# First k as plain f32, ReLU in DRAM token order, whole-tile stores: a Nystrom attention and squared-ReLU MLP kernel

## The chip, the cores and the metric

The kernel runs on one core of a Trainium2 chip. Its engines each run their own queue of instructions in order and wait for each other through semaphores: TensorE (PE, matmuls and their weight loads), VectorE (DVE), ScalarE (ACT), GpSimd (POOL) and SyncE (SP, which only issues transfers). PE writes into PSUM (8 banks of 2 KB for each of 128 partitions); DVE and ACT carry results from PSUM to the on-chip memory SBUF; DMA engines move data between DRAM and SBUF. Transfers can be issued from the queues of POOL, SP and ACT; only those from POOL's queue change the type on the way (f32 in DRAM to bf16 in SBUF) in this kernel.

The metric is the time of one execution in microseconds (us) on the device. Before the change it is 260.24 us, the median of three runs.

## The reference

Eight batches of eight heads, 576 tokens, head width 64. Nystrom attention with 32 landmarks, then an MLP with a squared ReLU:

```python
q_lm = q.reshape(B, H, m, S // m, D).mean(axis=3)
k_lm = k.reshape(B, H, m, S // m, D).mean(axis=3)
A  = sm(q, k_lm)        # sm: softmax of scale * a @ b^T
Bm = sm(q_lm, k_lm)
C  = sm(q_lm, k)
Z  = Bm.transpose(0, 1, 3, 2) / (norm1(Bm) * norminf(Bm) + 1e-06)
for _ in range(6):
    Z = 2 * Z - Z @ Bm @ Z
x = (A @ Z @ C @ v)     # heads side by side: (4608, 512)
h = x @ w_in            # (512, 2048)
r = np.maximum(h, 0.0)
out = (r * r) @ w_out   # (2048, 512)
```

All inputs and the output are f32; the kernel computes in bf16 with f32 sums.

## The kernel before

Everything is unrolled. The code adds each operation to a plan with its engine choices, and a table of numbers, `ORDER`, then emits the operations: each positive number names one operation, its engine and its PSUM bank; each negative one a run of matmuls of zeros (`fill`, L395), which compute nothing and keep TensorE running while it would wait. So the order of the instructions on every engine, and the choice between DVE and ACT, stand in that table alone; no cost is looked at when the kernel is built.

For each batch `attention(b)` and then `mlp_in(b)` and `mlp_out(b)` are planned, and the table interleaves the attention of the next batch with the MLP of this one. The parts and their lines:

- Loads. `load` (L333) brings q, k or v of a batch as bf16 through POOL's queue, with 96 partitions: partition p holds tokens 6p to 6p+5. `load_w_in` (L341) and `load_w_out` (L349) bring four pieces each of the weights on the same queue. k and q of batch 0 are its first two entries.
- Batch 0 and 1: k and q are transposed on TensorE (L521, evicted as `kqT`), later ones by a DMA transpose on SP's queue (L422).
- Landmarks: batch 0 by 24 matmuls with `seg` for each of k and q (L438), evicted as `kpart` and `qpart` (L273/L275) and folded (L451); later ones by L475.
- Bm and its softmax (L543 or L546, L559, L563, L567, L569), its transpose (L571) and scale (L586 to L592), the start `st` (L611, L613), six steps of a product on TensorE (L634 for batch 0, L639 later) and an update on DVE (L650), the last one into `zt` or `Zd` (L665, L658).
- C: products L679, row maximum L685, exponential L690 into `EC`, transposed (L702 for batch 0 and 1) into `ECT`; C times v (L730); with Z it gives `WT`.
- A: products L781, maximum and difference (`mxA` L790, `SA` L793), exponential L799 into `EA`, sums L805, scaling L816, transposed into `AT`.
- G = `WT` with w_in (L852), copied to SBUF; then the MLP: h from `AT` and G (L872, 4 matmuls of 288 columns for each of 16 blocks f), ReLU from PSUM into `r` (ACT L888 or DVE L890), its square into `gs` (ACT L897 or DVE L899), the output product (L936, 16 matmuls of 512 columns for each tile of 128 tokens), a copy to one of five buffers `o`, and the store to DRAM.

The columns of AT, `r` and `gs` stand in the order (c, p): column 96c + p is token 6p + c. A tile of 128 columns is therefore 128 tokens of which neighbours lie six rows apart in `out`, and it crosses from one c to the next: `store` (L911) issues two transfers for each tile (32 and 96 rows, or 64 and 64), all on SP's queue. The last tile is made in two halves of 256 columns.

```python
def relu(e, hk=hk, r=r):
    rj = r.rearrange("p (j t) -> p j t", j=2)
    src = two(hk)[:, :, 0:HALF]
```

Of the kernel before, what the change touches and what calls it, by code (L numbers as in the profile page):

```python
# [8 lines left out]
P = 128  # L9
# [5 lines left out]
F32 = mybir.dt.float32  # L15

B = 8
H = 8
# [216 lines left out]
def kernel(  # L235
# [111 lines left out]
    def load_w_out(j, gate=()):  # L347
# [8 lines left out]
        act_func_set_id=LN_EXP_SET, name=nc.get_next_instruction_name(),  # L356
        engine=mybir.EngineType.Activation, ins=[], outs=[]))

    load("k", 0)
    load("q", 0)  # L360

    seg = sb.tile([TP, M], BF16, name="seg")
# [553 lines left out]
    def mlp_out(b):  # L916
# [6 lines left out]
        for t, (sk, x0, pieces) in enumerate(tiles):  # L923
# [6 lines left out]
            for hp in range(parts2):  # L930
                for lo, hi in cuts:
# [19 lines left out]
                    if last:  # L951
                        store(osb, ("ob", on, lo), pieces, lo, hi)
# [52 lines left out]
```

## Time and profile before

| | us |
|---|---|
| median of 3 runs (260.06 to 263.48) | 260.24 |
| the profiled execution, whole | 258.97 |
| its span, first to last instruction | 257.3 |
| from the span's start to the first matmul that is not of zeros | 7.6 |
| from there to the first product of the MLP (L872) | 22.7 |
| from there to the last matmul | 222.2 |
| from there to the end of the span | 4.8 |

The granted clock of TensorE is 1.0 throughout. The profile is of one execution; the times of the table after the second row are cut out of its span. A busy share is an average over stages with different limits, so the stages are looked at one by one: ahead of the MLP the chain of batch 0 runs from engine to engine, in the long stage TensorE is busy nearly all the time, and at the end only stores are left. The DMA share of a stretch can be above 1, since reads and writes of the same engine overlap.

### The profile page before, as it was taken

How to read it: one execution, taken by the hardware profiler on the slowest of the kernel's cores; microseconds unless marked ns; L12 is line 12 of the kernel's file. 1: busy time of each engine (PE TensorE's matmuls, PEld its weight loads, DVE VectorE, ACT ScalarE, POOL GpSimd, SP SyncE). 2: the span in 40 equal slices, each digit the busy share in tenths (PEclk: the TensorE clock that was granted, in tenths of full speed). 3: DMA queues.
4: the chain of work that ended last, by engine and by line, in shares of the span. 5: the costliest groups of instructions: out<-in, count | busy, mean ns of one | idle time of the engine just before them, and what ended most of it. 6: DMA issues, size and time to landing. Idle time of an engine off the chain costs nothing.

```text
span 257.3 us, 7197 instructions
## 1 busy us (share of the span) xinstructions
PE 248.2 (96%) x2914; PEld 143.9 (56%) x2914; DVE 183.7 (71%) x423; ACT 179.1 (70%) x357; POOL 83.3 (32%) x127
## 2 busy tenths in 40 slices
PE   8988999999999999999999999999999999999992
PEld 3755645664655466546655665466645555555551
DVE  2396886779779988797578987766987676664400
ACT  1378999789954899786965895789697576454221
POOL 6253915415156224413351347225513220000000
PEclk9999999999999999999999999999999999999999
DMA  6999999799999999999979999999885108000425
GB/s 82 203 204 207 206 208 203 119 166 158 207 184 182 198 215 163 186 211 178 189 152 195 200 189 175 199 143 200 157 119 121 35 16 195 1 23 1 143 63 143
DMA packets 73345, 39.46 MB, mean 153 GB/s; under 512 B 46048, under 2 KB 68832, under 8 KB 73312
## 3 DMA queue, kind: packets, MB, share of 16 engines
q0 software_dynamic: 23040, 18.35, 47.7%
q1 hardware_dynamic: 50272, 20.65, 41.2%
q8 instruction: 23, 0.38, 0.5%
q14 instruction: 10, 0.08, 0.1%
HBM read 36.70 MB, written 9.44 MB: 179 GB/s over the span
## 4 chain that ended last, share of the span: by engine, by line
PE 77%; DMA 10%; DVE 4%; issue 3%; POOL 2%; ACT 2%; POOLq 0%; DVEq 0%; ACTq 0%
PE ps L936 43%; PE ps L872 21%; DMA kqraw<-in_k_dram 5%; DMA kqraw<-in_q_dram 5%; PE ps L852 3%; PE ps L475 2%; PE ps L781 2%; PE ps L730 1%; PE ps L639 1%; PE ps L521 1%; PE ps L395 1%; POOL EA L816 1%; ACT EC L690 1%; POOL Pd L578 1%; PE ps L492 1%
## 5 line engine op out<-in xcount | busy, mean ns | idle before, releaser
L936 PE MATMUL ps<-w_out_bf,gs 128*128 128x512 bf16 (+1 forms) x592 | 148.8, 374 | 0.0
L872 PE MATMUL ps<-AT,G 128*128 128x288 bf16 x512 | 79.1, 286 | 0.1
L936 PEld LDWEIGHTS <-gs 128*128 128x128 bf16 x592 | 53.9, 98 | 44.1 <-issue 5.2
L888 ACT ACTIVATE r<-ps 128x576 bf16<-128x576 f32 x84 | 53.5, 654 | 20.0 <-PE ps L872 13.1
L872 PEld LDWEIGHTS <-G 128*128 128x128 bf16 x512 | 49.0, 98 | 25.2 <-issue 0.7
L578 POOL TENSOR_TENSOR Pd<-st,ones_d 128x256 bf16<-128x256 bf16 x42 | 28.6, 682 | 79.6 <-DVE st L650 59.7
L897 ACT ACTIVATE gs<-r 128x576 bf16<-128x576 bf16 x70 | 45.5, 681 | 6.9 <-DVE r L890 6.5
L890 DVE TENSOR_SCALAR r<-ps 128x576 bf16<-128x576 f32 x44 | 32.7, 749 | 14.2 <-PE ps L872 10.4
L899 DVE TENSOR_TENSOR gs<-r 128x576 bf16<-128x576 bf16 x58 | 28.0, 498 | 3.6 <-ACT r L888 3.2
L267 ACT CAST G<-ps 128x512 bf16<-128x512 f32 x47 | 25.7, 590 | 6.5 <-PE ps L852 6.0
L267 ACT COPY o<-ps 128x512 f32<-128x512 f32 (+1 forms) x19 | 10.8, 576 | 15.6 <-PE ps L936 15.5
L650 DVE SCALAR_TENSOR_TENSOR st<-st,ps 128x128 bf16<-128x128 bf16 x40 | 11.3, 282 | 13.0 <-PE ps L639 8.0
L816 POOL TENSOR_TENSOR EA<-EA,rA 96x384 bf16<-96x384 bf16 x20 | 17.6, 890 | 8.8 <-DVE st L650 6.4
L269 DVE COPY o<-ps 128x512 f32<-128x512 f32 (+1 forms) x18 | 12.1, 669 | 10.3 <-PE ps L936 10.3
L790 DVE TENSOR_REDUCE mxA<-ps 96x16 f32<-96x512 f32 x24 | 16.1, 678 | 3.5 <-ACT gs L897 1.7
L793 DVE TENSOR_TENSOR SA<-ps,mxA 96x512 f32<-96x512 f32 x24 | 16.2, 680 | 0.3
L395 PE MATMUL ps<-zero 128*128 128x512 bf16 (+5 forms) x52 | 14.3, 400 | 1.3 <-DVE zero L401 1.3
L805 DVE TENSOR_REDUCE sA<-EA 96x24 f32<-96x768 bf16 x16 | 15.0, 940 | 0.4 <-ACT EA L799 0.3
L799 ACT ACTIVATE EA<-SA 96x512 bf16<-96x512 f32 x24 | 14.5, 626 | 0.7 <-DVE SA L793 0.7
L269 DVE CAST G<-ps 128x512 bf16<-128x512 f32 x17 | 11.4, 684 | 2.9 <-PE ps L852 2.5
L690 ACT ACTIVATE EC<-ps,nmc 128x576 bf16<-128x576 f32 x16 | 11.9, 744 | 2.1 <-DVE nmc L685 2.0
L685 DVE TENSOR_REDUCE nmc<-ps 128x1 f32<-128x576 f32 x16 | 11.8, 749 | 1.0 <-PE ps L679 1.0
(109 smaller groups left out, 237.4 us busy)
## 6 DMA issues: line engine op xcount, KB each, us to landing
kqraw<-in_k_dram POOLq DMA_DIRECT2D x8, 576.0 KB, 7.2
kqraw<-in_q_dram POOLq DMA_DIRECT2D x8, 576.0 KB, 11.5
vraw<-in_v_dram POOLq DMA_DIRECT2D x8, 576.0 KB, 9.0
out_dram<-o SPq DMA_DIRECT2D x23, 192.0 KB, 2.6
out_dram<-o SPq DMA_DIRECT2D x24, 128.0 KB, 2.5
w_in_bf<-in_moe_w_in_dram POOLq DMA_DIRECT2D x4, 512.0 KB, 9.8
w_out_bf<-in_moe_w_out_dram POOLq DMA_DIRECT2D x4, 512.0 KB, 10.6
out_dram<-o SPq DMA_DIRECT2D x23, 64.0 KB, 2.1
```

What stands on the lines that cost most here:

```text
L267: nc.scalar.copy(dst, src)
L269: ENG[e].tensor_copy(dst, src)
L395: mm(ps[:, bank, 0:64 * w], lhsT=zero[:, 0:P], rhs=zero[:, 0:64 * w], start=True, stop=True)
L578: ENG[e].tensor_tensor(dst[:], src.unsqueeze(2).to_broadcast([P, 2, NG, M]), ones_d[:].unsqueeze(1).to_broadcast([P, 2, NG, M]), ALU.mult)
L793: add({"DVE": dve(512)}, lambda e, sa=sa, j=j: nc.vector.tensor_tensor(grouped(SA[:, j, :]), grouped(one(sa)[0:TP, :]), mxA[:, j, :].unsqu ...
L816: ENG[e].tensor_tensor(w, w, rA[:, i, cs, :].rearrange("p c g -> p (c g)").unsqueeze(2) .to_broadcast([TP, NJ * NG, M]), ALU.mult)
L872: mm(t[:, j, 0:HALF], lhsT=G[:, i, f * P:(f + 1) * P], rhs=AT[:, i, j * HALF:(j + 1) * HALF], start=(i == 0), stop=(i == 1))
L888: nc.scalar.activation(rj, src, AF.Relu)
L890: nc.vector.tensor_scalar(out=rj, in0=src, scalar1=0.0, scalar2=None, op0=ALU.max)
L897: nc.scalar.activation(dst, r[:], AF.Square)
L899: nc.vector.tensor_tensor(dst, r[:], r[:], ALU.mult)
L936: mm(one(ok)[:, 0:hi - lo], lhsT=gs[:, f, x0:x0 + P], rhs=w_out_bf[:, f, lo:hi], start=(f == f0), stop=(f == f1 - 1))
```

## The change

It has four parts and a new table.

1. k of batch 0 is no longer POOL's first load. SP issues it as plain f32 in two halves of four heads each, into memory that `gs` uses later (`kf`); four casts of 96x768 make the bf16 `kqraw` of it, two on DVE and two on ACT. The landmark means of batch 0 (`means`) are split into halves of four heads, and the means and transposes of k wait only for their half. q of batch 0 becomes POOL's first load.
2. ReLU writes `r` with a stride: column 6t + 3j + c instead of (j, c, t), which is the order of tokens in DRAM. The square, `gs` and the output product then run over that order unchanged. The elements that one instruction writes one after another now stand 12 bytes apart.
3. A tile of 128 tokens is 128 neighbouring rows of `out`, and `store` issues one transfer for it.
4. For the last two tiles the table may also choose ACT's queue for a store; it does so once.

```diff
-    load("k", 0)
+    kf = gs.rearrange("p f s -> p (f s)")[0:TP, 0:2 * H * NC6 * D].bitcast(F32).rearrange(
+        "p (h c d) -> p h c d", h=H, c=NC6)
+
+    for y in range(2):
+        def load_kf(e, y=y):
+            nc.sync.dma_start(kf[:, 4 * y:4 * y + 4], k[0, 4 * y:4 * y + 4].rearrange("h (p c) d -> p h c d", c=NC6))
+
+        add({"SP": (450.0,)}, load_kf, writes=[("kf", y)], dma=(2.0 * H * S * D, 460.0, 700.0))
     load("q", 0)
+    for y in range(4):
+        def k_cast(e, y=y):
+            copy(e, kqraw[:, 0, 2 * y:2 * y + 2, :, :], kf[:, 2 * y:2 * y + 2])
+
+        add({"DVE": dve(768), "ACT": act(768, True)}, k_cast, reads=[("kf", y // 2), ("k", 0)], writes=[("kc", y)])
+    FIRST = {"k": [[("k", 0), ("kc", 2 * y), ("kc", 2 * y + 1)] for y in range(2)], "q": [[("q", 0)]] * 2}
...
-                add({"PE": pe(32, 24)}, means, reads=[(nm, 0), "seg"], writes=[mp], acq=("n", mp))
...
+                    add({"PE": pe(32, 12)}, means, reads=FIRST[nm][y] + ["seg"], writes=[mp],
+                        acq=None if y else ("n", mp))
...
-                    add({"PE": pe(TP, 12)}, tr, reads=[(nm, 0), "ident"], writes=[tp], acq=("h", tp))
+                    add({"PE": pe(TP, 12)}, tr, reads=(FIRST[nm][hf] if b == 0 else [(nm, 0)]) + ["ident"],
+                        writes=[tp], acq=("h", tp))
...
             def relu(e, hk=hk, r=r):
-                rj = r.rearrange("p (j t) -> p j t", j=2)
-                src = two(hk)[:, :, 0:HALF]
+                rj = r.rearrange("p (t j c) -> p j c t", j=2, c=NJ)
+                src = two(hk)[:, :, 0:HALF].rearrange("p j (c t) -> p j c t", c=NJ)
...
-    def store(osb, key, pieces, lo=0, hi=DM):
...
-                    nc.sync.dma_start(rows[a:a + m, tok, lo:hi], osb[p0:p0 + m, lo:hi])
...
+    def store(osb, key, row, lo=0, hi=DM, ends=False):
+        def go(e):
+            ENG[e].dma_start(out[row:row + P, lo:hi], osb[:, lo:hi])
...
-                store(osb, ("ob", on, 0), pieces)
+                store(osb, ("ob", on, 0), row, ends=b == B - 1 and t > 2)
```

The table is new from its first number to its last:

```diff
-    136, 24, 64, 104, 176, -1280, 880, 802, 928, 404, 448, 856, -197, 480, 528, -117, 962, 1040, 1016, 224, 608, 4344,
...
+    32, 336, 128, 72, 176, 104, 208, 256, 304, -640, 1080, 1128, 424, 602, -171, 640, 688, 1164, 1208, 376, -99, 722,
...
```

Three places of the order follow. The first is the start of ACT's queue before (`kqT_69` and `kqT_70` are the transposed k and q of batch 0 and of batch 1, `EC_99` and `EA_108` those of batch 0):

```order
L355 ACT_TABLE_LOAD
L267 COPY kqT_69<-ps 128x1152
L273 ACTIVATE kpart<-ps 128x256
L267 COPY kdup<-ps 128x256
L267 COPY kbd<-kdup 64x8x32
L267 COPY qdup<-ps 128x256
L563 ACTIVATE Eb,rs<-ps,nmb 128x32 x2
L799 ACTIVATE EA_108<-SA 96x2x2x128
L690 ACTIVATE EC_99,rsc<-ps,nmc 128x6x96 x2
```

And ACT's queue with the change, in the same place:

```order
L353 ACT_TABLE_LOAD
L265 COPY kqraw<-gs 96x768 x2
L265 COPY kqT_69<-ps 128x1152
L271 ACTIVATE kpart<-ps 128x256
L265 COPY kqT_69<-ps 128x1152
L271 ACTIVATE qpart<-ps 128x256
L265 COPY qdup<-ps 128x256
L265 COPY kqT_69<-ps 128x1152
L577 ACTIVATE Eb,rs<-ps,nmb 128x32 x2
L704 ACTIVATE EC_99,rsc<-ps,nmc 128x6x96 x2
```

The two casts of k (`kqraw<-gs`) came in ahead of everything; ACT now evicts three of batch 0's four transposes instead of one and `qpart` instead of `kdup`, and two of these evictions stand between `kpart` and `Eb`.

The second place is DVE's queue between the softmax of Bm of batch 0 and its first update (`st_93<-st_92`), before:

```order
L685 TENSOR_REDUCE nmc<-ps 128x1 x2
L567 RECIPROCAL rr<-rs 128x2
L790 TENSOR_REDUCE mxA<-ps 96x16
L569 TENSOR_TENSOR BB<-Eb,rr 128x64
L790 TENSOR_REDUCE mxA<-ps 96x16
L793 TENSOR_TENSOR SA<-ps,mxA 96x512
L571 STREAM_TRANSPOSE BTf<-BB 128x64
L793 TENSOR_TENSOR SA<-ps,mxA 96x512
L584 TENSOR_REDUCE cs<-BTf 128x2
L586 TENSOR_REDUCE mx<-cs 128x2
L589 TENSOR_SCALAR cc<-mx 128x2
L592 RECIPROCAL rc<-cc 128x2
```

And with the change:

```order
L699 TENSOR_REDUCE nmc<-ps 128x1 x2
L581 RECIPROCAL rr<-rs 128x2
L583 TENSOR_TENSOR BB<-Eb,rr 128x64
L804 TENSOR_REDUCE mxA<-ps 96x16
L585 STREAM_TRANSPOSE BTf<-BB 128x64
L804 TENSOR_REDUCE mxA<-ps 96x16
L598 TENSOR_REDUCE cs<-BTf 128x2
L807 TENSOR_TENSOR SA<-ps,mxA 96x512
L600 TENSOR_REDUCE mx<-cs 128x2
L733 RECIPROCAL rcv<-rsc 128x2
L603 TENSOR_SCALAR cc<-mx 128x2
L606 RECIPROCAL rc<-cc 128x2
```

One `SA` left this stretch; it and the last `mxA` follow after `st`, ahead of the updates.

The third place is the end of SP's queue (numbers behind `o` are the buffers), before:

```order
L911 DMA out_dram<-o_122 64x512
L911 DMA out_dram<-o_125 64x512 x2
L911 DMA out_dram<-o_121 32x256
L911 DMA out_dram<-o_121 96x256
L911 DMA out_dram<-o_124 32x512
L911 DMA out_dram<-o_124 96x512
L911 DMA out_dram<-o_121 32x256
L911 DMA out_dram<-o_121 96x256
```

And with the change, where the other half of the last tile is ACT's last instruction:

```order
L919 DMA out_dram<-o_125 128x512
L919 DMA out_dram<-o_122 128x512
L919 DMA out_dram<-o_124 128x512
L919 DMA out_dram<-o_123 128x512
L919 DMA out_dram<-o_121 128x256
```

One transfer stands for each tile or half tile. On TensorE the order holds 40 matmuls of zeros (17,792 columns) instead of 52 (23,680), 10 instead of 20 of them ahead of the first transpose; the means of q of batch 0 stand ahead of its transposes instead of behind them; and 24 products of L781 and 6 of L702 that stood ahead of the first L872 stand behind it.

More of the change, by code (lines that the diff above doesn't have):

```diff
@@ L432, in attention, with means @@
                 mp = (A, nm, "mp")
-                def means(e, raw=raw, mp=mp):
-                    t = one(mp).rearrange("p (h m) -> p h m", m=M)
-                    for h in range(H):
-                        for j in range(NJ):
-                            mm(t[:, h, :], lhsT=raw[:, h, 2 * j:2 * j + 2, :].rearrange("p c d -> p (c d)"),
-                               rhs=seg[:], start=(j == 0), stop=(j == NJ - 1))
-                add({"PE": pe(32, 24)}, means, reads=[(nm, 0), "seg"], writes=[mp], acq=("n", mp))
+                for y in range(2):
+                    def means(e, raw=raw, mp=mp, y=y):
+                        t = one(mp).rearrange("p (h m) -> p h m", m=M)
+                        for h in range(4 * y, 4 * y + 4):
+                            for j in range(NJ):
+                                mm(t[:, h, :], lhsT=raw[:, h, 2 * j:2 * j + 2, :].rearrange("p c d -> p (c d)"),
+                                   rhs=seg[:], start=(j == 0), stop=(j == NJ - 1))
+                    add({"PE": pe(32, 12)}, means, reads=FIRST[nm][y] + ["seg"], writes=[mp],
+                        acq=None if y else ("n", mp))
                 def means_ev(e, mp=mp, part=part, nm=nm):
@@ L918, in mlp_out @@
         if z == 0:
-            tiles = [("g", t * P, [(0, b, t * P, P)]) for t in range(4)]
+            tiles = [("g", t * P) for t in range(4)]
         else:
-            tiles = [("gx", DM, [(0, b - 1, DM, 64), (64, b, 0, 64)])]
-            tiles += [("g", S + 64 + t * P, [(0, b, 64 + t * P, P)]) for t in range(4)]
-        for t, (sk, x0, pieces) in enumerate(tiles):
+            tiles = [("gx", DM)] + [("g", S + 64 + t * P) for t in range(4)]
+        for t, (sk, x0) in enumerate(tiles):
+            row = (b - z) * S + x0
             parts2 = 2 if b == 0 else 1
@@ L951, in mlp_out @@
                     if last:
-                        store(osb, ("ob", on, lo), pieces, lo, hi)
+                        store(osb, ("ob", on, lo), row, lo, hi, ends=True)
             if not last:
-                store(osb, ("ob", on, 0), pieces)
+                store(osb, ("ob", on, 0), row, ends=b == B - 1 and t > 2)
     for j in range(4):
```

10 lines of the change are left out of this document (2 added, 8 removed), and 224 rows, old and new, of the table ORDER.

## The prediction

> **What bounds the kernel now.** I read the page first (span, busy shares, chain), then the stretches around the points where the program changes its nature, then single rows of the timeline at both ends.
>
> ```profile
> span 257.3 us, 7197 instructions
> ...
> PE 248.2 (96%) x2914; PEld 143.9 (56%) x2914; DVE 183.7 (71%) x423; ACT 179.1 (70%) x357; POOL 83.3 (32%) x127
> ...
> PE 77%; DMA 10%; DVE 4%; issue 3%; POOL 2%; ACT 2%; POOLq 0%; DVEq 0%; ACTq 0%
> ```
>
> TensorE is busy for 96% and is 77% of the chain. The view of stretches (length; busy time of PE, PEld, DVE, ACT, POOL with counts; clock; DMA share; GB/s) cuts the span where the first real matmul, the first L872 and the last matmul stand; the last row is the second stretch again with the zero matmuls of L395 alone.
>
> ```profile
> 0.00:7.57 7.57, 6.31 (x20) 2.35 (x20) 1.90 (x12) 1.28 (x1) 4.45 (x15) 1.00 0.72 100
> 7.57:30.28 22.71, 20.60 (x479) 14.18 (x479) 16.88 (x43) 16.65 (x38) 12.05 (x17) 1.00 1.28 205
> 30.28:252.50 222.22, 221.27 (x2419) 127.35 (x2416) 164.97 (x369) 160.83 (x319) 66.78 (x96) 1.00 0.87 150
> 252.50:257.30 4.80, 0.00 (x0) 0.00 (x0) 0.00 (x0) 0.37 (x1) 0.00 (x0) 1.00 0.46 129
> 7.57:30.28 22.71, 8.04 (x33) 2.53 (x32) 1.00 1.28 205
> ```
>
> So there are four parts. Up to 7.57 nothing real runs (6.31 us of zero matmuls while k is awaited). From 7.57 to 30.28, 8.04 of TensorE's 20.60 us are zero matmuls and 2.11 are idle: this is the latency chain of batch 0, and only 12.56 us are work. From 30.28 to 252.50 TensorE idles 0.95 us of 222.22. The last 4.80 us are copies and stores. No real matmul is removed, so the change can win only ahead of 30.28, in the tail, and at most 0.95 us between; it can lose anywhere.
>
> **The start.** Rows of the timeline (start, length, engine, what):
>
> ```profile
> 1.36 0.95 POOL L333 DMA_DIRECT2D kqraw<-in_k_dram  x1 [0.84 <-POOLq L989]
> 7.57 1.05 PEld L521 LDWEIGHTS <-kqraw 96*128 96x128 bf16 x24 [0.42 <-DMA kqraw<-in_k_dram]
> 8.30 1.12 ACT L267 COPY kqT<-ps 128x1152 bf16<-128x1152 bf16 x1 [6.21 <-PE ps L521]
> 9.40 0.39 ACT L273 ACTIVATE kpart<-ps 128x256 bf16<-128x256 f32 x1
> 10.47 1.05 PEld L521 LDWEIGHTS <-kqraw 96*128 96x128 bf16 x24 [0.41 <-DMA kqraw<-in_q_dram]
> 11.51 0.76 PE L438 MATMUL ps<-seg,kqraw 96*128 96x32 bf16 x24
> 19.34 0.78 ACT L267 COPY ECT<-ps 96x768 bf16<-96x768 bf16 x1
> 19.55 0.23 DVE L613 TENSOR_TENSOR st<-ps,rc 128x64 bf16<-128x64 f32 x1
> 27.20 0.22 DVE L665 SCALAR_TENSOR_TENSOR zt<-st,ps 128x64 bf16<-128x64 bf16 x1 [0.20 <-PE ps L634]
> 30.12 1.14 PE L872 MATMUL ps<-AT,G 128*128 128x288 bf16 x8
> ```
>
> And how transfers begin: the stretches in which k's first bytes flow on POOL's queue, the steady state, and a store on SP's queue with the stretches in which its bytes flow.
>
> ```profile
> 2.50:3.00 0.50, 0.50 (x3) 0.21 (x2) 0.00 (x0) 0.00 (x0) 0.50 (x1) 1.00 0.00 0
> 3.00:3.50 0.50, 0.50 (x3) 0.22 (x2) 0.00 (x0) 0.00 (x0) 0.42 (x3) 1.00 1.03 52
> 3.50:4.00 0.50, 0.50 (x3) 0.17 (x2) 0.29 (x3) 0.00 (x0) 0.43 (x3) 1.00 0.85 69
> 4.00:4.50 0.50, 0.50 (x3) 0.15 (x1) 0.24 (x2) 0.00 (x0) 0.39 (x3) 1.00 0.97 146
> 5.00:5.50 0.50, 0.50 (x3) 0.23 (x2) 0.23 (x1) 0.00 (x0) 0.50 (x2) 1.00 1.32 206
> 246.07 0.32 SPq L911 DMA_DIRECT2D out_dram<-o  x1
> 246.50:247.00 0.50, 0.50 (x5) 0.25 (x4) 0.00 (x0) 0.00 (x0) 0.00 (x0) 1.00 0.18 61
> 247.00:247.50 0.50, 0.50 (x5) 0.28 (x3) 0.00 (x0) 0.00 (x0) 0.00 (x0) 1.00 0.92 270
> kqraw<-in_k_dram POOLq DMA_DIRECT2D x8, 576.0 KB, 7.2
> ```
>
> (The last row is of the DMA issues: a tensor of one batch is 576 KB as bf16, so 1.18 MB as f32.)
>
> *When k and q arrive.* POOL's issue at 1.36 gives bytes at about 3.0 (1.65 us later), then 1.5 us of ramp at 52 to 146 GB/s against 206: (26 + 35 + 73) KB where 309 KB fit, 0.85 us lost. SP's issue at 246.07 gives bytes at about 246.85, 0.8 us later. If SP issues k at about 0.9, k flows from 1.7: 1.3 us earlier, and it fills q's ramp, 0.85 us more. q then lands at 10.47 - 2.15 = 8.3 at best. At worst plain f32 is written at the 206 GB/s of the cast transfer: k's 1.18 MB and q's 0.59 MB take 8.6 us from 1.7 and q lands at 10.3. The 270 GB/s of the store is a plain f32 transfer above 206, so I stay near the good end: q at 8.3, k's second half at 6.5 (once q's bytes flow the two share the engines; between 5.6 and 7.4).
>
> *The casts* (new, not in the trace): two of 96x768 on each of DVE and ACT. The nearest row is the 96x768 ECT copy on ACT, 0.78 us; DVE's fold copies now queue behind its casts, but fold is needed only after kpart. ACT's second cast ends at 6.5 + 0.8 = 7.3; its kqT copy (1.12) and kpart (0.39) follow to 8.8, against 9.79 now. The fold of k (0.3), 3.5 zero matmuls of 512 (0.22 each) and the means of q (0.76) end at 10.6, against 12.27. Two things make that: k comes earlier, and the means of q stand ahead of q's transposes (1.05 us of weight loads).
>
> *From there to L872.* C's products follow 1.45 us earlier, its two reductions on DVE too, and between those and st DVE has one SA (0.68) fewer: st at about 18.3 against 19.78. The landmark product L475 moves from before step 1 to after step 2, V's product to after step 5, but DVE now has a mxA, two SA, an ECT copy and a sum between the steps: I follow them to zt at 26.0, against 27.20 + 0.22. From zt to the first L872 are 2.9 us in the trace; the same operations stand there now. So L872 starts at about 28.6, 1.6 us earlier.
>
> *What that start no longer does.* Ahead of the first L872 stand 24 products of L781 and 6 of L702 fewer; they come later, where TensorE has no gap.
>
> ```profile
> 29.48 0.64 PE L781 MATMUL ps<-kbd,kqT 128*128 128x64 bf16 x16
> 17.66 0.50 PE L702 MATMUL ps<-ident,EC 128*96 128x128 bf16 x6
> ```
>
> 24 x 0.64/16 + 0.50 less two latencies of 0.15: 1.2 us given back. By this path the start wins 0.4 us. A second way: outside its 233.9 us of real work (248.2 - 6.31 - 8.04) TensorE spends, from the first real matmul to the last, 244.9 - 233.9 = 11.0 us; the order before has 26.25 zero matmuls of 512 there and the new one 24.75, 0.3 us less, and the first real matmul comes at about 5.6 instead of 7.57, so 2.3 us would be won. I take 1.2, bounds 3.0 won and 1.2 lost.
>
> **ReLU.** Strided writes of 2 bytes every 12 are not in the trace.
>
> ```profile
> L888 ACT ACTIVATE r<-ps 128x576 bf16<-128x576 f32 x84 | 53.5, 654 | 20.0 <-PE ps L872 13.1
> L890 DVE TENSOR_SCALAR r<-ps 128x576 bf16<-128x576 f32 x44 | 32.7, 749 | 14.2 <-PE ps L872 10.4
> 30.28:60.00 29.72, 29.72 (x353) 17.55 (x351) 23.56 (x61) 27.03 (x55) 12.28 (x18) 1.00 1.06 174
> 30.28:60.00 29.72, 11.15 (x18) 1.00 1.06 174
> ```
>
> Both read f32 from PSUM at some 1 ns an element (the L888 and L890 means over 576, less a fixed part), so no packed mode is lost; r is read back contiguous by the squares. I cost it at nothing; what covers it is slack, which the last two rows price: in the tightest stretch ACT is busy 27.03 of 29.72 us, 18 ReLUs of it (the second row is L888 alone). 2.69/18 = 0.15 us more for each uses the slack up.
>
> **Stores and tail.** 37 stores of whole tiles replace 74; rows stay 2 KB and bytes the same, so between 30.28 and 240 I count nothing (SP's queue also carries the transposes, which now wait behind fewer stores). At the end:
>
> ```profile
> 252.50 0.37 ACT L267 COPY o<-ps 128x256 f32<-128x256 f32 x1 [0.51 <-PE ps L936]
> 253.80 0.86 SPq L911 DMA_DIRECT2D out_dram<-o  x2
> 254.24 0.42 SPq L911 DMA_DIRECT2D out_dram<-o  x1
> out_dram<-o SPq DMA_DIRECT2D x2, 96.0 KB, 1.9
> ```
>
> The last copy ends at 252.87, but its two stores are issued at 253.80 and 254.24, behind others; the last lands 1.9 us later and the span ends 1.2 us after that. With one store for it, issued by an engine with nothing queued, that is 252.90 + 2.0 + 1.2 = 256.1 instead of 257.3: 1.2 us won. An issue from ACT isn't in the trace; by SP's 0.3 to 0.6 the gain lies between 0.9 and 1.6.
>
> **Sum.** 257.3 - 1.2 - 1.2 = 254.9 us of span. The profiled execution took 258.97, 1.67 more than its span, and lies 1.27 below the median of 260.24; taking 2.4 us from the median gives 257.8, say 258.0.
>
> **Rivals.**
>
> *k by SP brings nothing.* q lands at 10.3 as above, and only the moved products remain: +1.2 and -1.2, 260.2 us. For it: DMA is at its steady 205 GB/s all through 7.57 to 30.28, and both tensors must pass. Against: nothing flows before 3.0. The Trainium skill ("DMA: Bandwidth & Descriptors", section "Issuing engines are not separate DMA queues") says that transfers issued from several engines share the same engines, so that this saves only issue time; by it the sum is near this one. The trace agrees that the flow is shared, but shows 1.65 us to the first bytes on one queue and 0.8 on the other. Chance 0.20.
>
> *Slower: the strided writes cost.* Elements 12 bytes apart change a 16-byte line three times in four. If each change cost one more element time (1 ns or a little less), a ReLU would take 0.37 to 0.44 us longer; the point from which it decides is the 0.15 above. From 30.28 to 60 ACT would need 27.03 + 18 x 0.37 = 33.7 us in 29.72: 4 us lost there, and some 5 more in later stretches with less slack: 258 + 9 = 267 us. The Trainium skill ("Advanced Engine Details and Errata", section "SBUF Cachelines") has 16-byte lines and wants two hits on a line for full speed, which speaks against this change; no run here shows it. Against it: an engine that writes one element per ns need not write whole lines. Chance 0.13.
>
> *Faster.* Everything early holds (start 3.0), tail 1.6, the 0.95 us idle gone: 5.5 won, 254.7. Against: DVE's long operations between the steps. Chance 0.10.
>
> *The dense part stalls.* The new table spaces the ReLUs, squares and copies otherwise; a batch that waits on a load could give 4 us back, 262 us. The chain has one long load past the start, and there other work covered it, since TensorE idles only 0.95 us in all:
>
> ```profile
> 83.43 11.64 DMA kqraw<-in_q_dram
> ```
>
> Chance 0.07. The forecast itself keeps 0.50.
>
> **How the numbers follow.** The likeliest case gives 258.0. The range goes from 254.3 (all gains) to 263.5 (no early k, and a stall); outside lie most of the slower rival and the tip of the faster one. A measurement of this kernel tells about 2%, 5.2 us, from no change: below 255.0 is faster, above 265.4 slower. Most of the faster rival and a little of the forecast's own spread make 0.12; the slower rival and a stall that adds to the first rival make 0.14; 0.74 is left.
>
> **What would show it.** Right: bytes flowing from 1.7, q's means ending near 10.6, st near 18.3, the first L872 product near 28.6, ReLUs at 0.65 and 0.75 us, the last issue within 0.1 us of the last copy. Wrong: ReLU rows above 0.8 us with ACT at full share, k's second half after 8 us, idle TensorE between 30 and 250 us, or a tail still near 4.8.

## The result, and the profile after

| | before | after |
|---|---|---|
| median of 4 runs each, us | 261.1 (260.06 to 263.48) | 378.36 (374.85 to 382.42) |
| the profiled execution, us | 258.97 | 382.42 |
| its span, us | 257.3 | 380.6 |
| from its start to the first product of the MLP (L872, now L886) | 30.12 | 31.36 |
| from there to the last matmul | 222.4 | 345.6 |
| from there to the end of the span | 4.8 | 3.6 |

The ratio is 1.443, 95% interval 1.426 to 1.459: the change costs 117 us, and all of it lies in the long stage. The profiled execution is the slowest of the four, at a mean granted clock of 0.927 where the others had 0.941 to 0.945, and the ratio is taken without it. The prediction (258.0, 254.3 to 263.5) was wrong.

The page of the kernel after, the same lines as those shown of before; the last is the chain by line:

```profile
span 380.6 us, 7131 instructions
...
PE 283.2 (74%) x2902; PEld 153.4 (40%) x2902; DVE 242.5 (64%) x433; ACT 293.4 (77%) x351; POOL 82.7 (22%) x126
...
ACT 38%; PE 36%; DVE 13%; issue 8%; DMA 4%; SPq 0%; DVEq 0%; ACTq 0%
ACT r L902 31%; PE ps L944 20%; DVE r L904 10%; PE ps L886 8%; ACT gs L911 3%; DMA kqraw<-in_q_dram 2%; PE ps L866 2%; DMA gs<-in_k_dram 2%; PE ps L795 1%; PE ps L534 1%; ACT EA L813 1%; PE ps L488 1%; ACT o L265 1%; DVE gs L913 1%; PE ps L406 1%
```

TensorE fell from 96% to 74% of the span, and the chain, 77% TensorE before, goes through ScalarE and VectorE: 41% of it is ReLU (L902 and L904). The groups by line (busy us, mean ns of one, idle before it and its releaser), to be read against the two rows of L888 and L890 in the prediction, 654 and 749 ns:

```profile
L902 ACT ACTIVATE r<-ps 128x576 bf16<-128x576 f32 x84 | 171.0, 2156 | 26.2 <-PE ps L886 17.3 <-DVE gs L913 5.4 <-DVE mxA L804 1.8
L904 DVE TENSOR_SCALAR r<-ps 128x576 bf16<-128x576 f32 x44 | 90.5, 2089 | 23.3 <-PE ps L886 18.4 <-ACT gs L911 3.8 <-issue 0.6
L886 PE MATMUL ps<-AT,G 128*128 128x288 bf16 x512 | 85.7, 298 | 56.2 <-ACT r L902 40.2 <-DVE r L904 14.2 <-ACT BTc L265 1.1
```

One ReLU takes 2156 ns on ScalarE and 2089 on VectorE, three times what it took. Over 84 and 44 of them that is 126 and 59 us of work more. The h product (last row) stands idle for 56.2 us, nearly all of it until a ReLU has emptied a PSUM bank. The stretches (columns as in the prediction) of the long stage, of its first 30 us, and of those again with L902 alone:

```profile
31.36:377.00 345.64, 257.62 (x2443) 136.98 (x2441) 224.28 (x379) 273.68 (x315) 67.47 (x97) 0.93 0.53 98
31.36:61.36 30.00, 21.13 (x159) 12.09 (x158) 23.00 (x37) 25.70 (x31) 5.59 (x8) 0.89 1.00 165
31.36:61.36 30.00, 16.26 (x9) 0.89 1.00 165
```

In the first 30 us ScalarE gets through 9 ReLUs where before it did 18 in 29.72. TensorE is busy 21.13 us instead of 29.72. Its granted clock is 0.93 in the mean over the stage instead of 1.00, where the matmuls are 4 to 7% longer on top (L886 298 ns against L872 286, L944 400 against L936 374). That the pauses bring the clock down is not shown: in e6 below TensorE is busy for 98% of its span, and its mean clock is 0.79.

Rows of the timeline at the start and at the end of the same execution, then two of its stretches:

```profile
0.81 0.91 SPq L362 DMA_DIRECT2D gs<-in_k_dram  x2
8.05 0.83 ACT L265 CAST kqraw<-gs 96x768 bf16<-96x768 f32 x1 [1.60 <-DMA gs<-in_k_dram]
11.09 0.76 PE L450 MATMUL ps<-seg,kqraw 96*128 96x32 bf16 x24
18.25 0.22 DVE L627 TENSOR_TENSOR st<-ps,rc 128x64 bf16<-128x64 f32 x1
28.74 0.21 DVE L679 SCALAR_TENSOR_TENSOR zt<-st,ps 128x64 bf16<-128x64 bf16 x1
377.06 0.37 ACT L265 COPY o<-ps 128x256 f32<-128x256 f32 x1 [2.36 <-PE ps L944]
377.46 0.38 ACTq L919 DMA_DIRECT2D out_dram<-o  x1
```

```profile
1.50:2.00 0.50, 0.50 (x2) 0.15 (x1) 0.50 (x4) 0.50 (x1) 0.50 (x1) 1.00 0.27 43
22.00:28.00 6.00, 6.00 (x112) 3.96 (x111) 2.58 (x8) 4.64 (x7) 3.27 (x5) 0.50 1.24 207
```

K's bytes flow from 1.5 to 2.0 (forecast 1.7), its second half is cast at 8.05 (forecast landed at 6.5), the means of q end at 11.85 (10.6), st stands at 18.3 (18.3). Up to there the start is as forecast or up to 1.5 us behind it. From 22 to 28 us TensorE ran at a clock of 0.50 in this execution, and zt came at 28.7 (26.0). The same order in e4 below ran there at 1.00 and had zt at 25.5, and e11, with the table of before, has a clock of 0.50 from 24 to 30, so the fall is no sure mark of the change. At the end the last store leaves 0.03 us after the last copy, and 3.6 us pass behind the last matmul, as forecast.

### The profile page after: what moved, and what is told of

Its sections match the earlier page's. It is cut to its first block, busy times and chain, and to the rows that moved or that the text cites. A ratio compares the mean times of both kernels' runs of the same rounds, so it can differ in the third digit from the quotient of the medians.

```text
span 380.6 us, 7131 instructions
## 1 busy us (share of the span) xinstructions
PE 283.2 (74%) x2902; PEld 153.4 (40%) x2902; DVE 242.5 (64%) x433; ACT 293.4 (77%) x351; POOL 82.7 (22%) x126
## 4 chain that ended last, share of the span: by engine, by line
ACT 38%; PE 36%; DVE 13%; issue 8%; DMA 4%; SPq 0%; DVEq 0%; ACTq 0%
ACT r L902 31%; PE ps L944 20%; DVE r L904 10%; PE ps L886 8%; ACT gs L911 3%; DMA kqraw<-in_q_dram 2%; PE ps L866 2%; DMA gs<-in_k_dram 2%; PE ps L795 1%; PE ps L534 1%; ACT EA L813 1%; PE ps L488 1%; ACT o L265 1%; DVE gs L913 1%; PE ps L406 1%
## 5 line engine op out<-in xcount | busy, mean ns | idle before, releaser
L902 ACT ACTIVATE r<-ps 128x576 bf16<-128x576 f32 x84 | 171.0, 2156 | 26.2 <-PE ps L886 17.3
L944 PE MATMUL ps<-w_out_bf,gs 128*128 128x512 bf16 (+1 forms) x592 | 162.6, 400 | 7.2 <-ACT r L902 4.3
L886 PE MATMUL ps<-AT,G 128*128 128x288 bf16 x512 | 85.7, 298 | 56.2 <-ACT r L902 40.2
L904 DVE TENSOR_SCALAR r<-ps 128x576 bf16<-128x576 f32 x44 | 90.5, 2089 | 23.3 <-PE ps L886 18.4
L886 PEld LDWEIGHTS <-G 128*128 128x128 bf16 x512 | 51.4, 102 | 94.4 <-issue 74.2
L944 PEld LDWEIGHTS <-gs 128*128 128x128 bf16 x592 | 55.8, 102 | 56.9 <-issue 19.5
L911 ACT ACTIVATE gs<-r 128x576 bf16<-128x576 bf16 x68 | 46.6, 711 | 13.2 <-DVE r L904 12.6
L265 ACT CAST G<-ps 128x512 bf16<-128x512 f32 x42 | 23.1, 601 | 4.6 <-PE ps L866 4.4
L265 ACT COPY o<-ps 128x512 f32<-128x512 f32 (+1 forms) x25 | 14.9, 606 | 11.3 <-PE ps L944 11.1
L866 PE MATMUL ps<-w_in_bf,WT 64*32 64x512 bf16 x256 | 13.4, 432 | 12.2 <-ACT r L902 9.5
L267 DVE CAST G<-ps 128x512 bf16<-128x512 f32 x22 | 14.6, 683 | 6.5 <-PE ps L866 6.4
L267 DVE COPY o<-ps 128x512 f32<-128x512 f32 (+1 forms) x12 | 8.0, 674 | 11.2 <-PE ps L944 11.1
L592 POOL TENSOR_TENSOR BTd<-BTc,ones_d 128x256 bf16<-128x256 bf16 x7 | 5.2, 740 | 45.5 <-DVE BTc L267 28.0
```

The costliest lines, as they stand in the source:

```text
L265: nc.scalar.copy(dst, src)
L267: ENG[e].tensor_copy(dst, src)
L592: ENG[e].tensor_tensor(dst[:], src.unsqueeze(2).to_broadcast([P, 2, NG, M]), ones_d[:].unsqueeze(1).to_broadcast([P, 2, NG, M]), ALU.mult)
L866: mm(t[M * g:M * g + M, i, :], lhsT=WT[64 * i:64 * i + 64, g, :], rhs=w_in_bf[64 * i:64 * i + 64, g, n * 512:n * 512 + 512], start=True, s ...
L886: mm(t[:, j, 0:HALF], lhsT=G[:, i, f * P:(f + 1) * P], rhs=AT[:, i, j * HALF:(j + 1) * HALF], start=(i == 0), stop=(i == 1))
L902: nc.scalar.activation(rj, src, AF.Relu)
```

## The experiments

Twelve runs. First, whether it is the writing of ReLU at all, and what of it; then what is left when that is mended.

**e1: the change with the ReLU of before.** Two lines back:

```diff
-                rj = r.rearrange("p (t j c) -> p j c t", j=2, c=NJ)
-                src = two(hk)[:, :, 0:HALF].rearrange("p j (c t) -> p j c t", c=NJ)
+                rj = r.rearrange("p (j t) -> p j t", j=2)
+                src = two(hk)[:, :, 0:HALF]
```

> The changed kernel with ReLU writing r contiguously as before; all else, order table and one store per tile included, stays, so the rows of out are permuted. Theory W (the strided writes of ReLU are nearly the whole loss): ReLU back to 0.65 us on ScalarE and 0.75 on VectorE, 256 to 263 us. Theory O (the new order or the late k is to blame for much of it): above 290 us.

Measured: 264.77 us (262.62 to 266.33, 4 runs) against 260.98 of before on the same chip, ratio 1.012 (1.003 to 1.021). ReLU is back at 651 and 752 ns. So 113.6 of the 117 us go with these two lines. That is theory W, though the time lies 1.8 us above its range; what is left over before is looked at from e4 on.

**e2: before with the strided ReLU alone**, the opposite edit.

> The kernel before with the strided ReLU write alone; out's rows come permuted. Theory W: ReLU 2.1 us on both engines, 360 to 385 us. Theory O: below 300 us, since the old order spaces its work otherwise.

Measured: 386.31 us (one run, 1.3 us above theory W's range), ReLU 2160 and 2093 ns. The strided writing alone, with the old order, loads and stores, costs all that the change costs and more. The order, the stores and the first k are not needed to explain the loss.

**e3: the same 576 elements written with eight steps**, by block f.

```diff
-                rj = r.rearrange("p (t j c) -> p j c t", j=2, c=NJ)
-                src = two(hk)[:, :, 0:HALF].rearrange("p j (c t) -> p j c t", c=NJ)
...
+                step = (0, 1, 2, 3, 4, 8, 16, 48)[f % 8]
+                n = max(step, 1)
+                rj = r.rearrange("p (t j c) -> p j c t", j=2, c=n)
+                src = two(hk)[:, :, 0:HALF].rearrange("p j (c t) -> p j c t", c=n)
```

> The changed kernel with eight forms of the ReLU write, by block: contiguous and steps of 4, 8, 12, 16, 32, 64 and 192 bytes, each on a line of its own; the columns of r come permuted. Rival L (what costs is leaving a 16-byte line): contiguous 0.65 us, 4 bytes up to 1.0, 8 bytes about 1.5, 12 bytes 2.1, 16 bytes and more about 2.6. Rival A (any write of 2 bytes that does not continue the last one costs the same): all seven strided forms 2.0 to 2.2 us on both engines. Rival B (beyond lines, banks): the cost keeps growing from 16 to 192 bytes.

The rows of e3 by line; each form has its own. In this order: ScalarE contiguous, at steps of 4, 8, 12, 16 and 192 bytes; VectorE at 4 and 16:

```profile
L907 ACT ACTIVATE r<-ps 128x576 bf16<-128x576 f32 x12 | 8.2, 682 | 5.7 <-PE ps L886 5.4 <-ACT r L911 0.2
...
L911 ACT ACTIVATE r<-ps 128x576 bf16<-128x576 f32 x10 | 8.5, 847 | 4.5 <-PE ps L886 4.5
...
L915 ACT ACTIVATE r<-ps 128x576 bf16<-128x576 f32 x11 | 16.0, 1459 | 9.3 <-PE ps L886 8.9 <-ACT gs L944 0.2
...
L919 ACT ACTIVATE r<-ps 128x576 bf16<-128x576 f32 x11 | 23.5, 2137 | 3.1 <-PE ps L886 3.0
...
L923 ACT ACTIVATE r<-ps 128x576 bf16<-128x576 f32 x10 | 28.2, 2822 | 1.6 <-DVE gs L946 1.2 <-PE ps L653 0.4
...
L935 ACT ACTIVATE r<-ps 128x576 bf16<-128x576 f32 x11 | 31.6, 2870 | 5.0 <-PE ps L886 4.9
...
L913 DVE TENSOR_SCALAR r<-ps 128x576 bf16<-128x576 f32 x6 | 4.8, 808 | 3.8 <-PE ps L886 3.1 <-issue 0.6
...
L925 DVE TENSOR_SCALAR r<-ps 128x576 bf16<-128x576 f32 x6 | 16.6, 2761 | 0.7 <-ACT gs L944 0.2 <-PE ps L886 0.2
```

Up to 16 bytes the time grows with the step and beyond it stays (2643 ns at 32 bytes, 2749 at 64, 2870 at 192): the count of new 16-byte lines, 576 x step / 16, decides, and not the distance. From 8 to 12 bytes 144 lines cost 678 ns more, from 8 to 16 bytes 288 lines 1363: 4.7 ns a line both times. At 12 bytes 432 lines make 2.0 us. That is rival L of the expectation; its rivals A and B fall. The price is nearly five times the one that the prediction gave it, and VectorE pays it as ScalarE does (2761 ns at 16 bytes).

**e7: the same sweep with r kept as f32**, so that each step is twice as many bytes.

```diff
-    rts = [sb.tile([P, S], BF16, name="r%d" % i) for i in range(NR)]
+    rts = [sb.tile([P, S], F32, name="r%d" % i) for i in range(NR)]
```

> The eight forms of e3 with r kept as f32 instead of bf16: the same steps counted in elements (contiguous, 2, 4, 6, 8, 16, 32, 96), twice the bytes (8, 16, 24, 32, 64, 128, 384). It tells bytes from elements. Theory L (each new 16-byte line of the written tile costs about 4.7 ns): the step of 2 elements is 8 bytes, 288 new lines, and takes about 1.45 us where bf16 took 0.8; the step of 4 is 16 bytes and takes about 2.8 us where bf16 took 1.45; all wider steps take 2.65 to 2.85. Theory E (the step in elements is what costs): the same as in e3: about 0.83, 1.45, 2.1, 2.8, then flat. The contiguous form crosses 144 lines: at 4.7 ns for each 0.68 us, so little above the 0.68 and 0.80 of bf16 under either. The squares read f32 and are slower under both, which is no part of the test.

Rows of e7, ScalarE: contiguous, and steps of 8, 16 and 384 bytes:

```profile
L907 ACT ACTIVATE r<-ps 128x576 f32<-128x576 f32 x12 | 7.9, 660 | 2.9 <-PE ps L886 1.5 <-DVE gs L946 0.8 <-ACT r L911 0.6
...
L911 ACT ACTIVATE r<-ps 128x576 f32<-128x576 f32 x10 | 7.0, 701 | 2.4 <-PE ps L886 2.4
...
L915 ACT ACTIVATE r<-ps 128x576 f32<-128x576 f32 x11 | 13.3, 1211 | 5.0 <-DVE gs L946 2.8 <-PE ps L886 1.5 <-DVE mxA L804 0.6
...
L935 ACT ACTIVATE r<-ps 128x576 f32<-128x576 f32 x11 | 13.1, 1187 | 4.1 <-PE ps L886 4.0
```

Both theories failed. From 16 bytes on, where every element has a line of its own, all forms take 1148 to 1230 ns on ScalarE: the line still decides, but costs 2.1 ns (1211 / 576), not 4.7. At 8 bytes 288 lines at 2.1 ns are 0.6 us, which the stream of 576 elements hides. So a scattered bf16 pays more than twice what a scattered f32 pays.

**e10: bf16 again, in runs of x neighbours.** ReLU as in e3 with a last axis of x:

```diff
+                x, n = ((0, 0), (1, 3), (2, 1), (2, 2), (2, 3), (4, 1), (4, 3), (8, 3))[f % 8]
...
+                    rj = r.rearrange("p (t j c x) -> p j c t x", j=2, c=n, x=x)
+                    src = src.rearrange("p j (c t x) -> p j c t x", c=n, x=x)
```

> Eight forms of ReLU by block, all bf16, in runs of x neighbours that stand apart: x and the step from run to run: contiguous; 1 at 12 bytes; 2 (4 bytes) at 8, 16 and 24; 4 (8 bytes) at 16 and 48; 8 (16 bytes, a whole line) at 96. In e7 a new line cost 2.0 to 2.1 ns with f32 elements, in e3 4.7 ns with bf16. Theory H (a 2-byte piece of a 4-byte word has to be merged with what stands there, which is what makes it 4.7): whole words cost as f32 does: pairs at 16 bytes (288 lines) 0.6 us, so hidden under the stream: 0.65 to 0.8 us; pairs at 24 likewise; 1 at 12 bytes stays at 2.1. Theory T (any write of a bf16 stream to a new line costs 4.7 ns): pairs at 16 and 24 bytes take 1.45 us, quads at 48 bytes (144 lines) 0.75 to 0.85, runs of 8 at 96 bytes the contiguous time. Rows of out hold permuted tokens here.

Rows of e10, ScalarE: single elements at 12 bytes, pairs at 16 and at 24, runs of 8 at 96:

```profile
L914 ACT ACTIVATE r<-ps 128x576 bf16<-128x576 f32 x10 | 21.0, 2095 | 2.2 <-PE ps L886 1.4 <-DVE st L664 0.8
...
L922 ACT ACTIVATE r<-ps 128x576 bf16<-128x576 f32 x11 | 7.6, 693 | 3.4 <-PE ps L886 3.3
...
L938 ACT ACTIVATE r<-ps 128x576 bf16<-128x576 f32 x11 | 7.1, 647 | 4.9 <-PE ps L886 4.8
L926 ACT ACTIVATE r<-ps 128x576 bf16<-128x576 f32 x10 | 7.0, 698 | 0.8 <-PE ps L653 0.6 <-PE ps L886 0.2
```

Pairs change line 288 times, at 16 bytes as at 24, like the 8-byte step of single elements in e3, which took 1459 ns; they take 693 and 698. Theory T falls, and theory H stands: it is writing a 2-byte piece alone that makes a line cost 4.7 ns. That such a piece is merged with the word that holds it is the natural reading, but no run shows the merging itself.

**e4: the permutation on the reading side of ReLU.** r is written straight, in token order; the PSUM banks are read in steps. The output is that of the change.

```diff
-                rj = r.rearrange("p (t j c) -> p j c t", j=2, c=NJ)
-                src = two(hk)[:, :, 0:HALF].rearrange("p j (c t) -> p j c t", c=NJ)
+                rj = r.rearrange("p (t j c) -> p t j c", j=2, c=NJ)
+                src = two(hk)[:, :, 0:HALF].rearrange("p j (c t) -> p t j c", c=NJ)
```

> The changed kernel with the permutation moved to the reading side of ReLU: r is written contiguously in token order, and PSUM is read with steps of 96 and 512 f32 elements. Theory W (it is the writes into SBUF that cost): 0.65 to 0.8 us per ReLU and 256 to 264 us. Rival P (any stride in the access pattern costs, on either side): 2 us per ReLU and 370 us or more.

Measured: 261.66 us (260.61 to 266.83, 10 runs), ratio 1.0045 (0.9999 to 1.0092). The groups of ReLU in e4:

```profile
L902 ACT ACTIVATE r<-ps 128x576 bf16<-128x576 f32 x84 | 53.0, 648 | 22.7 <-PE ps L886 19.5 <-issue 1.1 <-DVE st L664 0.8
L904 DVE TENSOR_SCALAR r<-ps 128x576 bf16<-128x576 f32 x44 | 32.9, 752 | 17.5 <-PE ps L886 12.2 <-ACT gs L911 2.9 <-ACT EA L813 1.2
```

Its timeline at the end of the start, and two loads of batch 6:

```profile
25.48 0.20 DVE L679 SCALAR_TENSOR_TENSOR zt<-st,ps 128x64 bf16<-128x64 bf16 x1
28.45 0.65 PE L886 MATMUL ps<-AT,G 128*128 128x288 bf16 x4
...
133.47 0.81 POOL L331 DMA_DIRECT2D kqraw<-in_k_dram  x1 [0.49 <-issue]
141.79 0.81 POOL L331 DMA_DIRECT2D kqraw<-in_q_dram  x1
```

What its TensorE waits for (us in total, times, longest):

```profile
PE ps L488 <- DMA kqraw<-in_q_dram: 4.5, 2, 2.8
```

This strided read from PSUM costs nothing that the rows show: 648 and 752 ns, as before, and rival P falls. So the change's layout can be had from the other side of the same instruction. But 261.66 is not the forecast 258.0. The start is as forecast (28.45; 28.6), so is the tail (3.5 us), and the stage between is not: TensorE idles 6.7 of the 210 us from 30 to 240, against 0.9 before, most of it in the two waits of the means L488 for q, near 123 and 151.

**e6 and e5: the permutation at two other places**, as a reading of AT by TensorE and as a reading of r by the squares.

```diff
-                           rhs=AT[:, i, j * HALF:(j + 1) * HALF], start=(i == 0), stop=(i == 1))
+                           rhs=AT[:, i, :].rearrange("p (c t) -> p t c", c=NC6)[:, j * TP // 2:(j + 1) * TP // 2, :],
+                           start=(i == 0), stop=(i == 1))
```

> The changed kernel with the permutation put on TensorE: the moving operand of the product L887 reads AT in the token order of DRAM (steps of 192 bytes between neighbours of the stream), and ReLU copies straight. Same output as the changed kernel. Theory W (only writes pay for a new line): the product of 288 columns stays near 287 ns, ReLU is back at 0.65 and 0.75 us, and the time is near e4's, 261 to 265. Theory R (a read pays the same for a new line): 288 columns at 4.7 ns are 1.35 us for each of 512 products, about 1.07 us more than the 288 ns of e1, and the time goes above 700 us.

```diff
-                dst = gs[:, f, z * S:z * S + S]
+                dst = gs[:, f, z * S:z * S + S].rearrange("p (t c) -> p t c", c=NC6)
+                r = r.rearrange("p (c t) -> p t c", c=NC6)
```

> The changed kernel with the permutation one step later and on a reading side: ReLU writes r straight, the squares read r with steps of 192 bytes and write gs straight, in the token order of DRAM. Same output as the changed kernel. Theory R (reading another 16-byte line of SBUF for each 2-byte element costs ScalarE and VectorE what it cost TensorE in e6, where 288 columns took 264.0 / 512 = 516 ns instead of 78.9 / 512 = 154: 1.8 ns a column): the square by ScalarE goes from 680 ns to about 1.1 us, by VectorE, which reads r twice, from 480 ns to 1.1 to 2.1 us, and the time to 270 to 310 us. Theory F (their reads are free, as those of PSUM are in e4): ScalarE stays at 680 ns, VectorE at 480 to 750, and the time is near e4's, 261 to 266 us.

Measured: 486.22 and 297.1 us (one run each). The product of e6, and the squares of e5 by both engines:

```profile
L886 PE MATMUL ps<-AT,G 128*128 128x288 bf16 x512 | 264.0, 660 | 0.0
```

```profile
L912 ACT ACTIVATE gs<-r 128x576 bf16<-128x576 bf16 x68 | 78.7, 1186 | 5.4 <-DVE r L904 4.8
L914 DVE TENSOR_TENSOR gs<-r 128x576 bf16<-128x576 bf16 x60 | 71.5, 1209 | 4.0 <-ACT r L902 3.8
```

Reading SBUF line by line costs too: 264.0 / 512 = 516 ns for 288 columns, 1.8 ns a column, where 154 sufficed in e1 (78.9 / 512); 1186 / 576 = 2.1 ns an element on ScalarE (680 ns for the whole before) and the same on VectorE (480), which reads r twice in it. Theory R holds in e5 with its numbers. In e6 only its direction holds: it had 1.35 us for a product and over 700 us for the kernel. Four products of e6 in a row took 2.12 us where the clock was 0.50 (341 to 350 us) and 2.10 us where it was 0.90 (60 to 90 us), so the 1.8 ns do not come from the clock. The output products (L945) took 448 ns each instead of 374, so the 486 us are not the price of the reading alone.

**e8 and e9: the late loads.** In e4 the load of q at 141.79 stands on GpSimd's queue behind three masks that wait for VectorE. e8 moves its number in the table ahead of them; e9 moves the three loads of batch 5 as well.

```diff
-    ... 40624, 41224, 42368, 36936,
+    ... 40624, 44144, 41224, 42368, 36936,
...
-    38336, 39400, 40120, 40160, 37360, 33608, 41664, 44144, 43176, ...
+    38336, 39400, 40120, 40160, 37360, 33608, 41664, 43176, ...
```

> The kernel of e4 with one number of the order table moved: on GpSimd's queue the load of q for batch 6 stands right behind that batch's load of v again, ahead of the masks of BTd and Pd, as it does in the kernel before. Theory S (the late issue is what stalls the dense part: in e4 v is issued at 134.40 and q only at 141.79, the means L488 wait 2.8 us for it near 151, and the clock falls to 0.50 and 0.90 behind that): q is issued at about 135.2, has 14.5 us before it is wanted as against 14.9 in the kernel before, the wait of 2.8 us shrinks to under 0.5, the clock stays at 1.00 between 150 and 160, and the time is 3 us below e4 of the same chip: about 258.5. Rival T (the transfers themselves are the bound: the queue moves some 200 GB/s from 30 to 200 us, so an earlier issue lands no earlier): the wait near 151 stays above 2 us or comes up at another load, and the time stays within 1 us of e4's 261.7.

> e8 with the three loads of batch 5 also moved: they stand ahead of the two multiplications L830, the masks Zd and Pd on GpSimd's queue instead of behind them. In e4 those ran from 105.33 to 108.14 and the loads left at 108.14, 109.07 and 109.83; the means waited 1.7 us for q near 123. Theory S: the loads leave some 2.5 us earlier, the 1.7 us at 123 goes, and the time is 1.5 us below e8: about 257, which is 1 to 2% under the kernel before of the same chip. Rival T: no change against e8, because q lands when the queue has moved the bytes ahead of it.

Measured: e8 263.73 us (261.56 to 265.0), ratio 1.015 (1.008 to 1.023); e9 266.53 (264.06 to 269.54), ratio 1.023 (1.017 to 1.030). Neither is faster than e4. TensorE's longest wait in e8, and from e8's chain how long the moved load took (start, length):

```profile
PE ps L488 <- DMA kqraw<-in_q_dram: 3.9, 2, 2.2
```

```profile
136.65 15.95 DMA kqraw<-in_q_dram
```

The two longest waits of TensorE in e9:

```profile
PE ps L653 <- POOL Pd L592: 2.4, 1, 2.4
PE ps L886 <- DMA AT<-EA: 1.8, 1, 1.8
```

Theory S fell. In e8 q leaves 5 us earlier and then takes 15.95 us instead of e4's 10.59 (a row of e4's chain): it lands at 152.6, where it landed at 152.4. Rival T had that, though the time is 2 us above e4's and not within 1. In e9 the waits for q are down to 0.7 us, but the masks and the transpose of EA, which now stand or run behind the loads, are late instead. The load is late because what it must follow is late.

**e12: two buffers for the raw k and q**, and the loads of k for batches 3 to 6 further ahead on GpSimd's queue.

```diff
-    kqraw = sb.tile([TP, 2, H, NC6, D], BF16, name="kqraw")
+    kqraws = [sb.tile([TP, 2, H, NC6, D], BF16, name="kqraw%d" % i) for i in range(2)]
...
-                   writes=[(nm, b % 2 if nm == "v" else 0)], dma=(4.0 * H * S * D, 1500.0, 1000.0), gate=gate)
+                   writes=[(nm, b % 2)], dma=(4.0 * H * S * D, 1500.0, 1000.0), gate=gate)
```

> e8 with two buffers for the raw k and q instead of one, by turns of the batch, and the loads of k for batches 3 to 6 three to nine us further ahead on GpSimd's queue (ahead of the multiplications L830 instead of behind the masks that follow them). Theory L (a loop: three loads take 16.6 us from the issue of k to the landing of q, and the transposes that must be done before k may be overwritten 9.3 us more, 25.9 us together where TensorE's batch takes 24.4 to 26.5; with one buffer a late start is never won back): k's bytes move in the gap that the transposes left, q lands some 3 us earlier, the waits of 1.7 us near 123 and 2.2 us near 151 vanish, and the time is 258 to 259, 3 us under e4 and 0.99 of before. Rival D (the DMA engines are the bound, 160 to 193 GB/s from 30 to 180 us in e4 and 175 to 193 in before): the transposes get slower by what k's load takes, the waits come up again at L886 for AT or at the means, and the time stays at 261 to 264.

Measured: 260.14 us (258.98 to 261.9, 12 runs), ratio 0.997 (0.993 to 1.001); the profiled execution 258.98. Loads of e12 for batch 6:

```profile
128.48 0.81 POOL L331 DMA_DIRECT2D kqraw<-in_k_dram  x1
132.41 0.81 POOL L331 DMA_DIRECT2D vraw<-in_v_dram  x1
133.21 0.77 POOL L331 DMA_DIRECT2D kqraw<-in_q_dram  x1
```

The waits of TensorE for q, as the profile lists them, are gone, and the profiled time is what theory L said. The median lies 1 us above that, and the ratio forecast, 0.99, lies outside the interval. The waits that rival D wanted did not come up. Since the loads of k moved too, the share of the buffer alone is not shown. The loop itself shows in the rows of e8: with one buffer, k may only be loaded when the DMA transpose of the batch before is done.

```profile
125.56 5.58 SPq L433 DMA_TRANSPOSE kqT<-kqraw  x1
134.95 0.82 POOL L331 DMA_DIRECT2D kqraw<-in_k_dram  x1 [0.61 <-DMA kqT<-kqraw]
152.74 6.07 SPq L433 DMA_TRANSPOSE kqT<-kqraw  x1
```

The transpose takes 8.82 us (a row of e8's chain, 125.56 to 134.38), k's load is issued right behind it, q lands at 152.60, and the next transpose, which needs q, follows at 152.74: 27.2 us a round, with little in it but load and transpose. The same points in the kernel before:

```profile
119.71 5.74 SPq L422 DMA_TRANSPOSE kqT<-kqraw  x1
130.31 0.82 POOL L333 DMA_DIRECT2D kqraw<-in_k_dram  x1
145.99 6.20 SPq L422 DMA_TRANSPOSE kqT<-kqraw  x1
```

That is 26.3 us a round (the rounds of that kernel from 49 us on take 22.5 to 26.3), and TensorE waited for q for only 0.5 us in all.

**e11: the old table with the new stores and the reading of e4.** The kernel before, with only the layout and the stores of the change; ScalarE issues the last one.

```diff
+                rj = r.rearrange("p (t j c) -> p t j c", j=2, c=NJ)
+                src = two(hk)[:, :, 0:HALF].rearrange("p j (c t) -> p t j c", c=NJ)
...
+                    if first:
+                        ENG[e].dma_start(out[row:row + P, lo:hi], osb[:, lo:hi])
```

> The kernel before, with its order table and its loads, and of the change only two parts: the token order (written straight, read permuted from PSUM as in e4) and the stores (one for each output tile, 256 KB in DRAM order, the last half tile by ScalarE). Theory T (the table of the change sets the loads of q, k and v later, and DMA is too full to win it back: the two waits for q in e4 belong to the table): no wait for q above 0.7 us, the dense part as in before, and only the end gains, from 4.8 us behind the last matmul to 3.6: about 1.2 us under the kernel before of the same chip, ratio 0.995. Rival C (the contiguous stores, which move 381 to 389 GB/s at the end, take the DMA engines from the loads): q is waited for 2 us or more here too, and the time is at or above before, ratio 1.00 to 1.01.

Measured: 262.13 us (259.81 to 266.09, 12 runs) against 261.57, ratio 1.001 (0.997 to 1.006). TensorE's longest wait for a load:

```profile
PE ps L475 <- DMA kqraw<-in_q_dram: 2.2, 2, 1.6
```

The end is as it should be (3.2 us behind the last matmul instead of 4.8), and yet the time is that of before. In the profiled execution q is waited for 2.2 us, against 0.5 in before. The wait is on the side of rival C, but this is one execution, and one in which the start ran for 12 us at clocks of 0.64 and 0.51, so that the first product of the MLP came only at 34.2. From there to the last matmul it took 223.7 us, where before took 222.4. Theory T's gain of 1.2 us (0.995) is not there. Whether the contiguous stores slow the loads stays open.

## Why the prediction was wrong

**ReLU: the step that failed.** "I cost it at nothing; what covers it is slack", and the slack was worked out right: 0.15 us for each. The cost is 1.50 us on ScalarE (2156 - 654) and 1.34 on VectorE, ten times the slack, and e4, which differs from the change in nothing else, puts it at 378.36 - 261.66 = 117 us. The rival had the mechanism (three writes in four change a line, ScalarE is the engine that runs out, decided at 0.15 us) but took one element time, 1 ns, for a line change. e3 measured 4.7. It also stopped at the 30 us where slack was least and added "some 5 more" for the rest. With 1.5 us for each of 18 ReLUs in 29.72 us there is no stage with enough slack anywhere. The argument that put the rival at 0.13, that "an engine that writes one element per ns need not write whole lines", came from no row.

The Trainium skill ("Advanced Engine Details and Errata", section "SBUF Cachelines") gives the lines of 16 bytes, and the rule that two hits on a line are needed to hide the access. By that, a step of 12 bytes (1.33 hits on a line) must be slow and one of 8 bytes, two hits, fast. e7 agrees for f32: 701 ns at 8 bytes, 1211 at 16. For single bf16 elements e3 does not: 8 bytes, two hits, took 1459 ns, twice the contiguous time. The measurement decides, and no price stands on that page.

**The start** held as a sum and not in its first term. K's bytes begin where they should, but its second half came at 7.8 to 8.0 and not 6.5 in every run with the new table, while q's bytes flowed too, and the means of q ended at 11.85 where 10.6 was forecast: 0.4 us ahead of before's 12.27, not 1.7 (in e5, e6, e8 and e10 they ended at 13.0 to 13.2, behind before). What made that good must be the order of the work, though no run separates it: st came when forecast (18.3), zt in e4 half a us sooner (25.5 for 26.0), and the first product of the MLP at 28.45 in e4 and 29.12 in e12 (28.6).

**The rival that k by SP brings nothing** (0.20, 260.2 us) was therefore nearer than the forecast in that step: most of what the early load should have won is not there, and the 1.0 to 1.7 us by which the MLP begins earlier are close to the 1.2 that moved products alone explain. No run undid the load alone, so its share stays open.

**The tail** held: 3.6 us behind the last matmul in the change and 3.56 in e12, forecast 3.6.

**The long stage** was the second failure, hidden under the first. I took the idle time of 0.95 us as given and gave 0.07 to "a batch that waits on a load", priced at 4 us. That is about what e4 shows: waits of 4.5 us for q at batches 5 and 6. The load I quoted for it, at 83.43, was not the one. What I missed is the loop of load, transpose and load again through a single buffer, which takes about as long as TensorE's batch (27.2 us in e8). The new table starts it later, and e8 and e9 did not make that good by earlier loads; e12, with a second buffer and earlier loads of k together, removes the waits.

**The sum.** With both failures mended (e12) the profiled execution has 29.12 us of start, 224.6 of long stage and 3.56 of tail. Against before, that is 1.0 won, 2.2 lost and 1.2 won, together nothing. Of the 2.2, the products moved out of the start should account for about 1.2, by the prediction's own sum; no run shows that share by itself. Where the last 1.0 goes was not traced: the longest waits that e12's TensorE still has there are 0.8 us for ScalarE's `qdup` and 0.3 us. So even without its costly step the change does not win the 2.2 us that were forecast: e4 stands at 1.0045 of before, and e12, which adds to the change, at 0.997.

## What to carry to other kernels

When a layout must change on the way through SBUF, look at which side of which instruction takes the step: here the same permutation cost 117 us as a write of single bf16 elements, 35 us as a read of SBUF by the squares, 225 us (part of it by a lower clock) as a read of SBUF by TensorE, and nothing measurable as a read of PSUM. Price a new access pattern by a small sweep, or as a range with a high end, before you hide it behind slack; if the slack is 0.15 us and the price has no row, the chance of trouble is not 0.13. And look for loops through a single buffer (load, use, load again) whose length is that of the stage: here a new order that started one later was not caught up, and moving a single issue forward (e8) did not help.

## What the runs showed of the hardware that I had not expected

- A new 16-byte line of SBUF for each element costs ScalarE and VectorE 2.1 ns an element on writing f32 (e7). Reading bf16 at steps of 192 bytes costs them 2.1 ns an element too (e5), and TensorE 1.8 ns a column (e6); no run varies the step of a read.
- Writing one bf16 alone costs 4.7 ns for each new line (e3); a pair of neighbours costs hardly more than the stream (e10, ScalarE: 698 ns for 576 elements in pairs at 24 bytes, 662 contiguous).
- Reading f32 from PSUM in steps of 96 elements with a change of bank in each round cost nothing on ScalarE or VectorE: 648 and 752 ns in e4, 654 and 749 contiguous.
- Stores of whole tiles in DRAM order moved 381 and 389 GB/s at the end of the changed kernel (stretches from 376.5 to 377.5), where the prediction quotes 270 for rows six apart. It did not shorten the time (e11).
